# Five planner entries in an attention and two-layer feed-forward kernel: s rows ahead, v fetches later, small steps not held, sum fetches counted longer, A groups normalised ahead

## The chip, the cores and the metric

The kernel runs on one core of a Trainium2 chip. The metric is the device time of one execution in microseconds (us). Three runs of the kernel before gave 1052.65, 1056.55 and 1058.98 us; their median is 1056.55 us.

## The reference

Attention over 4 batches, 8 heads, 576 positions of 64 elements, with a causal mask and a bias from a running sum of `s`; its output, 2304 tokens by 512, goes through two gated feed-forward layers (512 to 1536 to 512), the first behind an RMS normalisation.

```python
cum  = np.cumsum(np.maximum(s, 0.0), axis=-1)
bias = -(cum[:, :, :, None] - cum[:, :, None, :])
scores = np.where(causal, -1e9, scale * q @ k.T + np.minimum(bias, 0.0))
attn = softmax(scores)                      # sum + 1e-9 in the denominator
x = (attn @ v), heads side by side          # 2304 x 512
xn = x / sqrt(mean(x * x) + 1e-6) * rms_g
h  = silu(xn @ w_gate) * (xn @ w_val);      x1 = h @ w_out
h2 = silu(x1 @ w2_gate) * (x1 @ w2_val);    out = h2 @ w2_out
```

## The kernel before, in words

**One planner writes every queue.** The kernel does not issue its instructions as it goes through its loops. Each `op(engine, ns, fn, r, w, pri, ...)` only records one instruction (or a few) with a planned duration, the buffers it reads and writes, and a priority. At the end `Plan.run` goes through a planned time: each time an engine is free, it takes the ready operation with the lowest `pri` number, and the order that comes out is the order of that engine's queue on the chip. On the chip each engine works through its queue strictly in that order and waits on semaphores, however the real times differ from the planned ones. So an entry that changes in one place can move other instructions of the same engine. The engines are TensorE (PE), VectorE (DVE), ScalarE (ACT), GpSimd (POOL) and SyncE (SP, which issues nearly all DMAs). Four entries matter here:

- `pri`: the rank. Attention unit number u has about `pri` u; its loads have u - 1000, and weight fetches of row f have 8 + 1.5 f - 1000. Matmuls of the first feed-forward layer have 10000 and more, so that they fill PE where attention leaves it free.
- `later`: planned ns by which the operation is held after what it depends on, unless that is a DMA.
- `slow`: for a DMA, ns that are added to its planned landing.
- `port`: a DVE operation with it is not planned to run while POOL runs one, nor does POOL begin one while it runs.

**The early part.** The first 256 positions ("group A") of the eight heads of batch 0 and then of batch 1 are computed by sixteen small units (`EarlyUnit`, `attend_early`). Each unit fetches q and k (L879, 128 KB), from the fifth unit on also a row of the bias (L884, 1 KB, from `cumA`) and v (L891, 64 KB; the first four units' v come over ACT's queue). It has scores on PE (L899, with L905 for the first four), a minimum and its column on DVE (L690), an exponent on ACT (L701), transposes (L917), a copy (L922 or L923) and the product with v (L927), copied to `x` (L932 or L933). There are four places for q and k and four for v, so unit u's fetches wait for unit u - 4. Weight fetches of the first layer (`raw`, L434, 512 KB each, two for each of the twelve rows of weights) share SP's queue; ACT, DVE and POOL turn what they bring into two halves H and L (L438, L440, L445 or L446, L449).

**Normalising a group.** When the eight heads of a group are in `x`, `normalise` squares them and sums the squares (L958, L965 in the early part; L958 to L991 later, where the squares are split and `split` is true), then comes a chain of small DVE operations on columns of 128 x 2 to 128 x 24 (helper `step`, L998; operations L1020 to L1054, of which the 18 from L1023 on form one chain: 6, then three rounds of 3, then 3), then transposes (L1058), a broadcast by matmul (L1066), the product (L1070) and the split into H and L (L1073, L1075). These are what the gate and value matmuls of the first layer (L1086) read, 24 for each row of weights and group.

**Later.** Batches 0 and 1 follow with their other positions ("group B"), batches 2 and 3 with both groups (`attend`, `units` numbered on). At their end `normalise` is called for each group with the rank of the last unit, less 1.0 for group A, less 2 inside. The second matmul of each layer is done by a scheme of seven products on sums of blocks. The sums of the first layer's rows are made by `sums_of_rows`: for each of six steps and two pairs of batches four fetches of h_d (L1365), four subtractions on DVE (L1370) and four stores (L1373).

Of the kernel before, what the change touches and what calls it, by code (L numbers as in the profile page):

```python
# [40 lines left out]
PE, DVE, ACT, POOL, SP, NONE = "PE", "DVE", "ACT", "POOL", "SP", "NONE"  # L41
# [38 lines left out]
class Plan:  # L80
# [20 lines left out]
    def op(self, eng, ns, fn, r=(), w=(), pri=0.0, later=0, port=False, slow=0.0):  # L101

        n = len(self.ops)
        done = 0
        if eng == SP:  # L110
            took = ns / self.RATE
            ns = max(450.0, took)
            done = 2300.0 + took - ns + slow
        deps, shared = set(), []
        for accesses, writes in ((r, False), (w, True)):
            for a in accesses:
                buf, part = a if isinstance(a, tuple) else (a, None)
                key = buf if isinstance(buf, str) else buf.key
                live = self.live.setdefault(key, [])
                keep = []  # L120
                for part2, m, wrote in live:
                    meets = part is None or part2 is None or part == part2
                    if meets and (writes or wrote) and m != n:
                        deps.add(m)
                    if not (writes and meets and (part is None or part == part2)):
                        keep.append((part2, m, wrote))
                keep.append((part, n, writes))
                self.live[key] = keep
                if not isinstance(buf, str) and buf.share is not None and buf not in shared:
                    shared.append(buf)  # L130
                    buf.uses += 1
        engs = eng if isinstance(eng, list) else [(eng, ns)]
        self.ops.append((engs, fn, deps, pri, done, shared, later, port))
        return n
# [160 lines left out]
TINY = 70  # L295
# [5 lines left out]
def tile_kernel(  # L301
# [16 lines left out]
    op = plan.op  # L318
# [83 lines left out]
    P_CONV, P_MOE, P_ATT = -1.0e3, 1.0e4, 0.0  # L402
# [72 lines left out]
    cumA = buf("at", "pTB1", [P, 2 * P], F32, "cumA")  # L475
# [372 lines left out]
    class EarlyUnit(Unit):  # L848
# [28 lines left out]
        def load(self, pri):  # L877
            ql, i = self.ql
            op(SP, 8 * D * 256, lambda en: en.dma_start(  # L879
                out=ql()[0:D, :, 288 * i:288 * i + 256], in_=qk[self.b, self.h, 0:D, :, 0:256]),  # L880
               w=self.parts[:2], pri=pri)
            n = self.b * NH + self.h
            if not self.first:
                op(SP, 1024, lambda en: en.dma_start(  # L884
                    out=ql()[D:D + 1, 1, 288 * i:288 * i + 256], in_=cumA()[n:n + 1]),
                   r=[cumA, self.rows], w=self.parts[2:], pri=pri, later=1000)
            if self.first:
                op(ACT, 450, lambda en: en.dma_start(
                    out=self.v(), in_=vp[self.b, self.h, :, 0:2]), w=[self.vl], pri=pri - 1e6)
            else:  # L890
                op(SP, 512 * P, lambda en: en.dma_start(  # L891
                    out=self.v(), in_=vp[self.b, self.h, :, 0:2]), w=[self.vl], pri=pri)

        def scores(self, pri):
            for t in self.tiles:
# [44 lines left out]
    def normalise(i, g, tot, pri, split=True):  # L940
# [3 lines left out]
        x = xbuf[i]  # L944
# [11 lines left out]
        for k in range(KD):  # L956
# [3 lines left out]
               r=[(x, (k, 0)), (x, (k, 64))], w=[q], pri=pri)  # L960

            if not split:
                def sums(en, q=q, k=k):
# [9 lines left out]
                    out=qh()[:, :n], in0=q()[:, :n], scalar1=1.0, scalar2=1.0, op0=ALU.mult,  # L973
                    op1=ALU.mult)}, r=[q], w=[qh], pri=pri)
            op([(DVE, c_tt(n)), (POOL, c_ptt(n))], 0, lambda en, q=q, qh=qh: en.tensor_tensor(
                out=sqL()[:, :n], in0=q()[:, :n], in1=f32(qh()[:, :n]),
                op=ALU.subtract), r=[q, qh], w=[sqL], pri=pri, port=True)
# [6 lines left out]
        if split:  # L984
# [3 lines left out]
               r=[ps], w=[sq[0]], pri=pri)  # L988
            ps2 = mo_bank()
            for c in range(nt):  # L990
                op(PE, C_TR, lambda en, c=c: en.transpose(  # L991
                    ps2()[:, c * P:c * P + P], sq[0]()[:, at[c]:at[c] + P], ident()),
                   r=[sq[0], ident], w=[ps2], pri=pri)
# [3 lines left out]

        def step(fn, r=(), w=None):  # L998
            w = [col] if w is None else w
            op(DVE, TINY, fn, r=[*w, *r], w=w, pri=pri, port=True)  # L1000

        def m():
            return col()[:, 0, :nt]
# [30 lines left out]
        for _ in range(3):  # L1034
# [6 lines left out]
            out=over(), in0=over(),  # L1041
# [118 lines left out]
    def attend(b, gs, xs):  # L1160

        tots = [totals[2 + b] if b < 2 else totals[2 * (b % 2) + x] for x in xs]
        for pair in range(NH // 2):
            heads, last = [], []
            for z in range(2):
                h = 2 * pair + z
                hd = Head(b, h, S, 0 if "A" in gs else 256)
                heads.append(hd)
                for g, x, tot in zip(gs, xs, tots):
                    units.append(hd)  # L1170
                    pri = P_ATT + len(units) - 1
                    if g == gs[0]:
                        hd.load(pri - 1000)
                        hd.prep_qk(pri - 0.5)
                        hd.prep_v(pri - 0.4)
                    u = Unit(hd, g, x, tot)
                    if g == "A":
                        u.scores(pri)
                        u.values(pri + 0.4)
                        continue  # L1180
                    last.append(u)
                    if z:
                        both = PairTile(heads, tot3[b % 2])
                        both.load(pri - 1000)
                        both.scores(pri - 0.1)
                    u.scores(pri)
            both.turn(pri + 0.1)
            last[0].values(pri + 0.2)
            both.second(pri + 0.3)
            last[1].values(pri + 0.4)  # L1190
        both.sums(tots[-1], P_ATT + len(units))
        for g, x, tot in zip(gs, xs, tots):
            normalise(x, g, tot, P_ATT + len(units) - (1.0 if g == "A" else 0.0))

    attend_early(0, 0, totals[0])
    attend_early(1, 1, totals[1])
# [157 lines left out]
    def h_rows(gi, f):  # L1354
        return [(f"h_d{gi}", (f, lo)) for lo in sorted(h_parts[gi])]
# [3 lines left out]
    def sums_of_rows(p, k, pri, after=()):  # L1359

        n = 512
        b11, b12, b21, b22 = t_bufs
        for t, gi, f in ((b11, 2 * p, k), (b12, 2 * p + 1, k), (b22, 2 * p + 1, k + K6),
                         (b21, 2 * p, k + K6)):
            op(SP, 4 * P * n, lambda en, t=t, gi=gi, f=f: en.dma_start(out=t(), in_=h_d[gi][f]),  # L1365
               r=[*h_rows(gi, f), *after], w=[t], pri=pri, later=2000)
        for i, (out, a, b) in enumerate(((b11, b12, b11), (b12, b22, b12), (b22, b22, b11),
                                         (b21, b21, b22))):
            op(DVE, c_tt(n) + 60, lambda en, out=out, a=a, b=b:
               en.tensor_tensor(out=out(), in0=a(), in1=b(), op=ALU.subtract), r=[a, b], w=[out],  # L1370
               pri=pri, port=True)
            name = ("T1", "T3", "T2", "T4")[i]
            op(SP, 4 * P * n, lambda en, out=out, name=name: en.dma_start(  # L1373
                out=t_d[p, name][k], in_=out()), r=[out], w=[(f"t{p}{name}", k)], pri=pri)
# [527 lines left out]
```

## Time and profile before

| what | value |
|---|---|
| median of three runs | 1056.55 us |
| profiled execution, its own time | 1057.39 us |
| its span | 1055.6 us |
| mean granted TensorE clock | 0.997 |
| PE / DVE / ACT / POOL busy | 99% / 73% / 61% / 26% of the span |
| DMA moved | 211.17 MB, 200 GB/s on average |

The span runs from the first instruction to the last. Busy is the time in which an engine has an instruction at work; a matmul's end is modelled. The granted clock is the share of TensorE's full clock (2.4 GHz); 0.50 is 1.2 GHz. A letter q after an engine (SPq) is its issuing part. "L899" is a line of the kernel.

### The profile page before, as it was taken

To read this page: it belongs to the slowest core of one execution; us is meant where nothing else is said; L and a number is where in the kernel's file an instruction comes from. 1 tells how busy PE (TensorE), PEld (TensorE's weight loads), DVE (VectorE), ACT (ScalarE), POOL (GpSimd) and SP (SyncE) were. 2 spreads that over 40 slices of the span, in tenths; PEclk is the share of its full clock that TensorE was granted. 3 is DMA by queue.
4 is the path that set the end of the run, shared out by engine and by line. 5 is a ranking of instruction groups with operands and counts; after the bars stand their busy time and mean duration, and the time that the engine had idled before them with its cause. 6 is when DMAs were issued, how large, how long until landed. Compare 5 with 4: busy or idle time off the path is not lost.

```text
span 1055.6 us, 19496 instructions
## 1 busy us (share of the span) xinstructions
PE 1040.2 (99%) x6322; PEld 937.2 (89%) x6322; DVE 771.7 (73%) x1880; ACT 641.5 (61%) x1373; POOL 273.5 (26%) x370
## 2 busy tenths in 40 slices
PE   8899999999999999999999999999999999999998
PEld 6599999999999999999988889888888888888888
DVE  7699788777777776757779887665667766976462
ACT  6689778867664775333466865555556444665652
POOL 4368556544343542000000000212122221300000
PEclk9899999999999999999999999999999999999999
DMA  7797555534546732666697662666667667888673
GB/s 204 229 282 221 144 150 148 164 117 128 158 142 204 246 106 85 188 208 206 206 299 244 197 222 84 222 210 220 228 202 256 219 232 263 292 259 261 207 244 105
DMA packets 127959, 211.17 MB, mean 200 GB/s; under 512 B 16176, under 2 KB 55600, under 8 KB 127856
## 3 DMA queue, kind: packets, MB, share of 16 engines
q1 hardware_dynamic: 126656, 209.32, 62.8%
q8 instruction: 50, 0.82, 0.3%
q10 hardware_dynamic: 1200, 0.60, 0.2%
q14 instruction: 53, 0.43, 0.1%
HBM read 145.29 MB, written 64.56 MB: 199 GB/s over the span
## 4 chain that ended last, share of the span: by engine, by line
PE 79%; DMA 7%; DVE 6%; ACT 3%; issue 3%; POOL 1%; SPq 1%; ACTq 0%; POOLq 0%; DVEq 0%
PE mo L1086 21%; PE mo L1455 8%; PE mo L1626 8%; PE sps L1626 6%; PE tp L1455 6%; PE sps L1455 5%; PE tp L745 4%; PE tp L733 3%; PE sps L664 2%; PE mo L1702 2%; DMA raw<-in_w_gv 2%; PE sps L1086 2%; PE tp L1086 2%; PE mo L1510 2%; DMA lq<-cumA 1%
## 5 line engine op out<-in xcount | busy, mean ns | idle before, releaser
L1086 PE MATMUL mo<-xL,H 128*128 128x256 f32 (+1 forms) x672 | 201.8, 300 | 0.1
L1086 PE MATMUL mo<-xH,H 128*128 128x256 f32 (+1 forms) x672 | 200.7, 300 | 0.3
L1086 PE MATMUL mo<-xH,L 128*128 128x256 f32 (+1 forms) x672 | 200.2, 298 | 0.0
L1351 DVE TENSOR_TENSOR hL<-hh,hH 128x512 fp32r<-128x512 f32 (+1 forms) x192 | 125.2, 662 | 67.1 <-ACT hH L1348 66.4
L1348 ACT ACTIVATE hH<-hh 128x512 fp32r<-128x512 f32 (+1 forms) x192 | 115.2, 603 | 91.6 <-DVE hL L1351 21.3
L1086 PEld LDWEIGHTS mo<-xL,H 128*128 128x128 f32 x672 | 127.0, 189 | 1.0 <-POOL xL L1075 0.5
L1086 PEld LDWEIGHTS mo<-xH,H 128*128 128x128 f32 x672 | 126.7, 189 | 1.1 <-ACT xH L1073 0.6
L1086 PEld LDWEIGHTS mo<-xH,L 128*128 128x128 f32 x672 | 126.9, 189 | 0.2
L701 ACT ACTIVATE sc<-sc,col 128x128 f32<-128x128 f32 (+3 forms) x128 | 73.2, 572 | 48.4 <-DVE col L690 46.1
L1455 PE MATMUL mo<-hH,wo 128*128 128x512 f32 x312 | 97.8, 389 | 0.0
L1455 PEld LDWEIGHTS mo<-hH,wo 128*128 128x128 f32 x312 | 58.6, 188 | 12.2
L1455 PE MATMUL mo<-hL,wo 128*128 128x512 f32 x156 | 61.1, 391 | 0.2 <-DVE hL L1351 0.2
L1455 PE MATMUL tp<-hH,wo 128*128 128x512 f32 x192 | 60.4, 389 | 0.0
L1093 ACT ACTIVATE t<-mo 128x256 f32<-128x256 f32 (+1 forms) x84 | 33.9, 403 | 43.4 <-PE mo L1086 43.3
L1632 ACT ACTIVATE u<-sps 128x512 f32<-128x512 f32 x48 | 28.5, 593 | 50.6 <-PE sps L1626 48.8
L745 PE MATMUL tp<-pTB,vst 128*128 128x320 f32 (+2 forms) x320 | 52.2, 294 | 1.6 <-ACT pTB L736 1.0
L1455 PE MATMUL sps<-hH,wo 128*128 128x512 f32 x168 | 52.9, 389 | 0.0
L1095 DVE SCALAR_TENSOR_TENSOR t<-t,mo 128x256 f32<-128x256 f32 (+1 forms) x84 | 37.8, 450 | 19.4 <-ACT t L1093 19.1
L738 DVE TENSOR_TENSOR pTB<-tp,pTB 128x512 fp32r<-128x512 f32 x64 | 44.0, 687 | 8.3 <-ACT pTB L736 7.2
L745 PEld LDWEIGHTS tp<-pTB,vst 128*128 128x128 f32 x320 | 46.5, 189 | 3.6 <-ACT pTB L736 1.7
L1589 POOL TENSOR_TENSOR tmp<-x,x 128x512 f32<-128x512 f32 x2 | 2.9, 1454 | 178.5 <-DVE x L1471 178.5
L733 PE MATMUL tp<-ident,sc 128*128 128x128 f32 x304 | 46.9, 274 | 0.6 <-DVE x L754 0.4
(289 smaller groups left out, 2925.9 us busy)
## 6 DMA issues: line engine op xcount, KB each, us to landing
raw<-in_w_gv SPq DMA_DIRECT2D x44, 511.8 KB, 5.4
tb<-h_d SPq DMA_DIRECT2D x48, 256.0 KB, 3.9
t<-tb SPq DMA_DIRECT2D x48, 256.0 KB, 2.4
hh<-t SPq DMA_DIRECT2D x48, 256.0 KB, 3.1
lq<-in_qk SPq DMA_DIRECT2D x32, 288.0 KB, 3.6
cb<-cum_d SPq DMA_DIRECT2D x32, 288.0 KB, 3.9
hh<-h_d SPq DMA_DIRECT2D x36, 256.0 KB, 3.6
h_d<-hh SPq DMA_DIRECT2D x54, 128.0 KB, 2.3
```

The lines of the kernel that those rows point to most:

```text
L701: op(ACT, c_act(o + m, 2) + 35, lambda en: en.activation(sc()[:m, :o + m], sc()[:m, :o + m], ACTF.Exp, scale=-1.0, bias=col()[:m, 0, t:t + 1],
L733: op(PE, C_TR, lambda en, pt=pt, a=a, kb=kb, t=t: en.transpose(pt()[:, a * P:a * P + P], self.sc[t]()[:, kb * P:kb * P + P], ident()), r=[ ...
L738: op(DVE, c_tt(n), lambda en, pt=pt, c=c: en.tensor_tensor(out=place(L, c), in0=source(pt, c), in1=f32(place(H, c)), op=ALU.subtract), r=[ ...
L745: op(PE, c_mm(n), lambda en, w=w, z=z, kb=kb, d0=d0, n=n, o=o: en.matmul(po()[:, o:o + n], vst[j]()[:, kb, :], pT[g][z]()[:, d0:d0 + n], s ...
L1086: op(PE, c_mm(n), lambda en, a=a, x=x, c=c, k=k, i=i: en.matmul(ps()[:, :n], a()[:, c], x()[:, k, :n], start=(k == 0 and i == 0), stop=(k ...
L1093: op(ACT, c_act(n), lambda en: en.activation(t()[:, :n], gp()[:, :n], ACTF.Tanh, scale=0.5), r=[gp], w=[t], pri=pri)
L1095: op(DVE, c_tt(n), lambda en: en.scalar_tensor_tensor(out=t()[:, :n], in0=t()[:, :n], scalar=1.0, in1=gp()[:, :n], op0=ALU.add, op1=ALU.mu ...
L1348: op(ACT, c_act(n) + 35, lambda en: en.activation(H(), src(), ACTF.Copy), r=[src, *after], w=[H], pri=pri)
L1351: lambda en: en.tensor_tensor(out=L(), in0=src(), in1=f32(H()), op=ALU.subtract),
L1455: op(PE, c_mm(n), lambda en, m=m, w=w, xx=xx, kk=kk, i=i: en.matmul(ps[m]()[:, :n], w(), xx(), start=first and kk == 0 and i == 0, stop=kk ...
L1626: op(PE, c_mm(n), lambda en, w=w, xx=xx, cut=cut, kk=kk, i=i: en.matmul(ps()[:, :n], W[w]()[:, cut], xx(), start=first and kk == 0 and i == 0,
L1632: op(ACT, c_act(n), lambda en: en.activation(dst(), ps()[:, :n], ACTF.Copy), r=[ps], w=[dst], pri=-1.0e4)
```

## The change

Five entries of the planner's records change; no instruction does.

```diff
--- before.py
+++ after.py
@@ EarlyUnit.load
                 op(SP, 1024, lambda en: en.dma_start(
                     out=ql()[D:D + 1, 1, 288 * i:288 * i + 256], in_=cumA()[n:n + 1]),
-                   r=[cumA, self.rows], w=self.parts[2:], pri=pri, later=1000)
+                   r=[cumA, self.rows], w=self.parts[2:], pri=pri - 3, later=1000)
...
                 op(SP, 512 * P, lambda en: en.dma_start(
-                    out=self.v(), in_=vp[self.b, self.h, :, 0:2]), w=[self.vl], pri=pri)
+                    out=self.v(), in_=vp[self.b, self.h, :, 0:2]), w=[self.vl], pri=pri + 2.2, later=800)
@@ normalise, step
-            op(DVE, TINY, fn, r=[*w, *r], w=w, pri=pri, port=True)
+            op(DVE, TINY, fn, r=[*w, *r], w=w, pri=pri, port=split)
@@ attend
-            normalise(x, g, tot, P_ATT + len(units) - (1.0 if g == "A" else 0.0))
+            normalise(x, g, tot, P_ATT + len(units) - (4.0 if g == "A" and len(gs) > 1 else 0.0))
@@ sums_of_rows
             op(SP, 4 * P * n, lambda en, t=t, gi=gi, f=f: en.dma_start(out=t(), in_=h_d[gi][f]),
-               r=[*h_rows(gi, f), *after], w=[t], pri=pri, later=2000)
+               r=[*h_rows(gi, f), *after], w=[t], pri=pri, later=2000,
+               slow=2500)
```

The row of the bias of early unit u now ranks with the q and k of unit u - 3, and its v with those of unit u + 2.2, held for 800 ns after the place is free. The two early groups are normalised with `split` false, so their small steps lose `port`; the later groups keep it. Group A of batches 2 and 3 is normalised with a rank three units lower. Each fetch of `sums_of_rows` has a planned landing 2.5 us later.

## Rows read from the trace of the kernel before

**Rows 1.** The page, busy us, share of the span and instructions of TensorE.
```profile
PE 1040.2 (99%) x6322; PEld 937.2 (89%) x6322; DVE 771.7 (73%) x1880; ACT 641.5 (61%) x1373; POOL 273.5 (26%) x370
```

**Rows 2.** Windows: stretch, length, busy us (instructions) by engine, clock, DMA share, GB/s.
```profile
26.00:53.00 27.00, 23.07 (x118) 15.96 (x119) 19.08 (x73) 17.79 (x53) 8.22 (x9) 0.87 0.74 230
...
38.30:45.10 6.80, 6.79 (x21) 4.49 (x22) 2.67 (x12) 2.08 (x8) 1.94 (x2) 0.50 0.53 154
45.10:51.20 6.10, 5.45 (x36) 3.97 (x34) 5.39 (x17) 4.96 (x14) 1.59 (x2) 1.00 0.99 344
...
53.00:73.00 20.00, 19.72 (x154) 18.76 (x152) 18.66 (x57) 18.37 (x42) 12.18 (x14) 1.00 0.89 275
73.00:93.00 20.00, 19.63 (x154) 19.08 (x155) 19.19 (x61) 17.86 (x42) 16.53 (x22) 1.00 0.74 242
...
280.00:300.00 20.00, 18.77 (x134) 17.97 (x133) 16.01 (x63) 13.48 (x35) 8.56 (x15) 1.00 0.60 173
```

**Rows 3.** Chain of waits: start us, us, what the chain goes through.
```profile
31.70 6.48 DMA lq<-cumA
...
63.61 8.25 DMA raw<-in_w_gv
...
286.08 5.96 DMA tb<-h_d
```

**Rows 4.** Timeline of PE, 33 to 52 us: start, us, instruction, idle before.
```profile
38.31 0.77 PE L899 MATMUL sps<-lq 128*128 128x128 f32 x2 [2.48 <-DMA lq<-cumA]
...
44.30 1.25 PE L927 MATMUL tp<-pTA,vl 128*64 128x256 f32 x4
...
51.24 0.57 PE L1086 MATMUL mo<-xH,H 128*128 128x256 f32 x2
```

**Rows 5.** Timeline of SP, 28 to 44 us: DMAs in order of issue.
```profile
29.91 0.43 SPq L434 DMA_DIRECT2D raw<-in_w_gv  x1
30.38 0.55 SPq L879 DMA_DIRECT2D lq<-in_qk  x1
31.33 0.33 SPq L891 DMA_DIRECT2D vl<-in_vp  x1
```

**Rows 6.** DMA issues at 30.40 and at 31.35 us: KB, us to landing.
```profile
lq<-in_qk SPq DMA_DIRECT2D x1, 128.0 KB, 7.3
...
vl<-in_vp SPq DMA_DIRECT2D x1, 64.0 KB, 6.6
```

**Rows 7.** Timeline of DVE: small steps of normalise, first, second and a later group.
```profile
30.22 0.17 DVE L1023 TENSOR_TENSOR fac<-mo,fac 128x16 f32<-128x16 f32 x1
...
35.10 0.16 DVE L1038 SCALAR_TENSOR_TENSOR rc<-rc 128x2 f32<-128x2 f32 x1
...
48.07 0.18 DVE L1054 TENSOR_TENSOR sq<-fac,sq 128x16 f32<-128x16 f32 x1
...
66.75 1.25 DVE L1028 TENSOR_SCALAR rc<-rc 128x2 f32<-128x2 f32 x1
...
91.06 0.27 DVE L1054 TENSOR_TENSOR sq<-fac,sq 128x16 f32<-128x16 f32 x1
...
321.49 0.18 DVE L1023 TENSOR_TENSOR fac<-mo,fac 128x24 f32<-128x24 f32 x1
...
325.55 0.18 DVE L1054 TENSOR_TENSOR sq<-fac,sq 128x24 f32<-128x24 f32 x1
```

**Rows 8.** Timeline of POOL, 61 to 92 us.
```profile
66.54 1.43 POOL L619 TENSOR_TENSOR kLL<-lq,kHH 128x576 fp32r<-128x576 f32 x1
```

**Rows 9.** Timeline of PE, 305 to 331 us: transposed factors, then broadcast.
```profile
306.53 0.38 PE L1058 MATMUL mo<-ident,sq 128*128 128x128 f32 x2
...
326.33 0.96 PE L1066 MATMUL mo<-xL,sel 128*128 128x256 f32 x4
```

**Rows 10.** Waits of SP, 26 to 60 us, and DVE: us, times, longest.
```profile
SPq L891 <- PE tp L927: 2.5, 1, 2.5
...
DVE tb L1370 <- DMA tb<-h_d: 5.5, 5, 2.3
```

## The prediction

> **What bounds the kernel now.** I read the page's busy times first, then the windows by stage, then the chain of waits, then the timelines of single engines where the chain leaves TensorE. TensorE (PE) is busy 1040.2 of the 1055.6 us of the span [rows 1], so an edit can only gain where PE is idle, where its matmuls are few, or where its clock is low. The windows say where that is: from 53 to 73 us PE has 19.72 busy us in 20 with 154 matmuls, but from 26 to 53 us only 23.07 in 27 with 118, and the granted clock there is 0.87 [rows 2]. The first 53 us are the early part: sixteen short units of attention (eight heads of batch 0, eight of batch 1), a latency chain with nothing to fill PE beside it, since the first gate/value matmul (L1086) comes only at 51.24 us [rows 4]. From there PE is full, and whatever moves PE work ahead of 51 us shortens the whole run by the same amount as long as PE stays full behind it.
>
> Three things hold that part up. The chain of waits shows a row of s that is issued at 31.70 us and takes 6.48 us to land [rows 3]; PE stands still for 2.48 us until it is there and starts again at 38.31 us [rows 4]. From 38.30 to 45.10 us the granted clock is then 0.50 [rows 2], that is 1.2 GHz instead of 2.4, after the stall and a stretch of few matmuls. And the group of eight heads that is complete at 30 us is normalised only at 48 us: its 18 small VectorE (DVE) steps begin at 30.22 us, the twelfth of them runs at 35.10, the last at 48.07 [rows 7]. Later PE is idle in one more place that the diff touches: 1.23 us between 280 and 300 us [rows 2], where the chain has a fetch of h_d that takes 5.96 us [rows 3].
>
> **The change part by part.** No instruction is added or removed; five entries of the planner change, so what changes is the order of each engine's queue. I work against the profiled execution, 1057.39 us (span 1055.6 and 1.8 around it), which is 0.84 above the median of the runs, 1056.55.
>
> *Small early steps not held back (port=split).* So far the planner let no such step begin while it had GpSimd (POOL) at work, nor the other way round. The same chain of steps with POOL idle shows what it takes unheld: from 321.49 to 325.55 us, 4.1 us from first to last [rows 7]. In the early part other DVE work lies between, and the first twelve took 4.9 us; at that pace all 18 take some 7.3 us and end near 37.5 us instead of 48.2. Behind the last step the matmuls began 3.2 us later (48.07 to 51.24), so the first would come near 41 us, ten earlier. What that is worth: between 38.30 and 51.20 us PE did 21 + 36 = 57 matmuls [rows 2]; at the rate of the next stage (154 in 20 us, 0.13 us each) it would be 99. 42 matmuls are 5.5 us; from 41 us on, 10.2 of the 12.9 us, it is 4.3. I take **-4.0**, bounds 0 (the steps stay behind the units' own DVE work) and -5.5. The second group's chain, which ends only at 91.06 us [rows 7], shortens as well, but PE is full there (idle 0.28 of 20 us from 53, 0.37 from 73) [rows 2]: **-0.5**, bounds 0 and -0.65.
>
> What it costs: a step may now meet a POOL operation. One did already: at 66.75 us a step of L1028, a tiny operation like those of 0.16 us, took 1.25 us, and ended with the POOL subtraction of L619 that ran from 66.54 for 1.43 us [rows 7, 8]. DVE works in order, so the next scores of the units stand behind such a step. At worst all 18 meet one so: 18 x 1.1 = 20 us of DVE time a group; at best the order before already paid as much, and nothing is lost. I take 0, since the other steps in these rows took 0.16 to 0.27 us, and the planner's times, by which the hold works, drift from the chip's anyway; this stays a rival below. The Trainium skill (SBUF — State Buffer, "Who interferes with whom") states this as a lock: a DVE instruction with two SBUF inputs, or in a two-port mode, and a POOL instruction that reads SBUF exclude each other, the later one waiting for the whole of the earlier. The row of L1028 agrees with it. By that rule, with POOL busy 8.22 of 27 us before 53 us and 16.53 of 20 us from 73 [rows 2], a third to five sixths of the steps are held up, by half a POOL operation (0.7 us), an estimate of 4 to 11 us of DVE a group; if a quarter of that reached PE, the sum below would be -5 to -3 instead of -6.
>
> *Rows of s ahead (pri - 3), v later (+2.2 and 800 ns).* Twelve rows of 1 KB and twelve fetches of v of 64 KB on SP's queue change places among themselves and with the weight fetches (raw, 512 KB). The queue's order shows in [rows 5]: a weight fetch at 29.91, the q/k of the unit that stalls at 30.38, a v at 31.33, then the row at 31.70. A row ahead of that v would still stand behind the weight fetch, and so does q/k, which lands 7.3 us after its issue [rows 6], at 37.7 us: only 0.5 us before the row (38.18). The fetch of weights ranks ahead of this q/k before and after the change. So the stall of 2.48 us shrinks by 0.5, not by all: **-0.5**, bounds 0 and -2.5 (the weight fetch itself slips behind).
> A v whose slot is not yet free blocks SP, and the weight fetches behind it: 2.5 us in one case between 26 and 60 us [rows 10]. A later v lets those fetches pass. The price is a v that lands late. The v of 31.33 us lands 6.6 us later [rows 6], at 37.9, and its unit's value matmuls begin at 44.30 [rows 4]: 6.4 us of cover, 3 us less if the units run ahead by that much. One weight fetch put ahead costs what the spacing of landings shows, at most the 6.5 us of a whole landing. I take 0, bounds 0 and +3.
>
> *Longer fetches counted for first sums (slow=2500).* The 24 + 24 fetches of h_d get a planned landing 2.5 us later, so their subtractions (L1370) are placed later in DVE's queue. DVE waited for them 5.5 us in all, 2.3 at the longest [rows 10], and that once is behind the fetch of 5.96 us, where PE ran dry: all idle time of that window is 1.23 us [rows 2]. I take **-1.0**; bounds -1.23 and +0.8 (buffers are held longer, and another fetch is late instead). The sums are needed from 521 us, so their delay is covered.
>
> *Late first groups normalised ahead (-4 for -1).* Two groups have it, batches 2 and 3. The first shows why it is worth nothing: its factors are transposed at 306.53 us, yet its broadcast (L1066) starts at 326.33 [rows 9], because the matmuls of the earlier batch still read the tiles it writes. Ranked three units higher it waits longer at the same place. **0**, bounds -0.8 and +0.8 (it holds one of four PSUM banks earlier).
>
> Sum: -4.0 - 0.5 - 0.5 - 1.0 = -6.0, so 1057.4 - 6.0 = **1051.4 us**. If PE were short of work behind 51 us the early gain would be given back; 53 to 93 us says it is not.
>
> **The rivals.**
> *Given back.* Matmuls that start ten us earlier need weights, and the chain has a wait for a weight fetch at 63.61 us, 8.25 us long [rows 3]. For it: one megabyte is wanted for each pair of matmul rows, and the DMA share is 0.89 from 53 to 73 us [rows 2]. Against it: PE was idle only 0.28 us there, and the second group, normalised sooner, lets each weight serve twice. Then only the sums and the 0.5 us of the row are left, less some reordering: 1054.5 to 1058, say 1056.
> *The edit doesn't reach the chip.* The stall at 38 us comes from transfers that the planner takes to be quicker than they are, and steps planned behind the stalled unit's scores stand still with it. Then the last six steps end where they did, about 47 us, and the gain is 1 to 2 us: 1055.5.
> *Slower: v behind weight fetches.* In its place in SP's queue a v finds one or two weight fetches ahead; its unit's value matmuls stand at PE's head, and all behind them waits. It decides when a v lands later than its transposes are done, so when the cover of 6.4 us is used up: 3 us by faster units, the rest by a fetch (4 to 6.5 us). One such stall would be like the one seen: 2.5 us, and the clock falls again, 6.8 us at half for up to 3.4 us. If the old stall also stays, 1057.4 + 5.9 - 1.0 = 1062. Against it: one v in twelve has to be hit so, and with moving matmuls as fill the clock need not fall.
> *Slower, by DVE.* Each blocked small step (1.1 us) delays the units' scores; between 53 and 93 us DVE is busy 18.66 and 19.19 of 20 us [rows 2], so ten such blocks are 10 us of that stage's DVE. PE has fill meanwhile, and so only a part counts: 1058 to 1062.
>
> **How the numbers follow.** Forecast, 1048 to 1054.5: 0.52. Given back or not reached, 1054.5 to 1059: 0.27. The two slower rivals, 1059 to 1064: 0.14. More than forecast (also the 2.48 us stall gone and the clock not fallen), below 1048: 0.07. The range 1046 to 1060 leaves out the upper half of the slow cases and the best of the good ones. A measurement of this kernel tells about 0.5% from no change: faster ends at 1051.3 us, slower begins at 1061.8. The forecast lies on the first bound; of its case somewhat over two thirds lie under it, since the bounds of the largest term reach further down: faster 0.44, same 0.45, slower 0.11.
>
> **What would show it.** Right: the last small step of the first group before 40 us and the first L1086 matmul near 41; no 0.50 clock after 42 us; more than 57 matmuls between 38.3 and 51.2; the wait for the row gone or near 2 us; no long wait of DVE for tb (L1370). Wrong: L1086 still starts near 50 us; PE waits for vl (L927) anywhere before 60 us; small steps of more than 1 us in numbers; PE idle over 0.6 us in 20 between 53 and 93 us; gaps behind 300 us that were not there.

## The result, and the profile after

The changed kernel takes 1067.56 us (median of six runs, 1063.62 to 1068.64), the kernel before 1054.17 beside it: ratio 1.0113, 95% interval 1.0087 to 1.0139. The forecast of 1051.4 had the wrong sign, and the time lies outside its range. The profiled execution took 1068.64 us, 11.25 more than that of before. From the page, TensorE's busy time:

```profile
PE 1045.5 (98%) x6322; PEld 941.4 (88%) x6322; DVE 788.3 (74%) x1887; ACT 643.0 (60%) x1376; POOL 263.1 (25%) x360
```

The same 6322 matmuls; the busy time grew by 5.3 us [rows 1], some 3 us of it because more of them ran at half clock (the mean granted clock was 0.994 instead of 0.997; an estimate), and the rest of the 11.25 us is idle time. The windows say where (columns as in [rows 2]; the stretches of that group first, then three longer ones):

```profile
26.00:53.00 27.00, 25.08 (x138) 18.65 (x137) 20.15 (x79) 19.96 (x63) 8.94 (x11) 0.87 0.74 212
38.30:45.10 6.80, 6.50 (x25) 4.95 (x26) 2.48 (x12) 2.93 (x9) 2.75 (x3) 0.61 0.91 286
45.10:51.20 6.10, 6.10 (x38) 4.97 (x37) 5.02 (x15) 5.34 (x17) 3.16 (x5) 0.88 0.50 147
53.00:73.00 20.00, 19.32 (x145) 17.75 (x143) 18.46 (x43) 14.36 (x33) 11.16 (x13) 1.00 0.87 277
73.00:93.00 20.00, 15.72 (x109) 15.00 (x108) 19.65 (x59) 15.78 (x37) 12.40 (x17) 0.91 0.79 237
...
53.00:106.00 53.00, 46.90 (x344) 44.14 (x343) 50.60 (x129) 40.35 (x93) 33.80 (x40) 0.97 0.76 233
106.00:350.00 244.00, 241.51 (x1795) 236.43 (x1794) 195.65 (x670) 173.31 (x437) 113.96 (x184) 1.00 0.52 149
540.00:600.00 60.00, 57.71 (x251) 46.32 (x250) 48.64 (x78) 38.99 (x70) 1.30 (x1) 1.00 0.79 258
```

The same three long stretches of the kernel before, and one that is used below:

```profile
53.00:106.00 53.00, 52.35 (x409) 50.57 (x408) 50.30 (x158) 47.67 (x112) 40.76 (x50) 1.00 0.81 252
106.00:350.00 244.00, 241.52 (x1802) 236.76 (x1801) 188.35 (x656) 170.78 (x433) 116.88 (x188) 1.00 0.51 151
540.00:600.00 60.00, 59.98 (x263) 49.00 (x263) 51.17 (x82) 40.16 (x71) 1.30 (x1) 1.00 0.78 248
...
350.00:1050.00 700.00, 699.07 (x3865) 615.72 (x3864) 493.96 (x921) 386.55 (x722) 94.92 (x97) 1.00 0.66 213
```

Ahead of 53 us the change did a little of what the forecast says: 25 + 38 = 63 matmuls between 38.3 and 51.2 us instead of 57. Behind it, from 53 to 106 us, PE does 65 fewer; at 0.13 us each that is 8.5 us. It is idle 6.1 us there (53 - 46.90) instead of 0.65, while DVE is as busy as before. Between 540 and 600 us another 2.3 us are lost.

TensorE's timeline of the changed kernel: the stalled unit, the first transposed factors, the first gate/value matmul, and the longest stall behind it (in brackets the idle time before and what ended it):

```profile
38.60 0.46 PE L899 MATMUL sps<-lq 128*128 128x128 f32 x2 [1.92 <-DMA lq<-in_qk]
...
44.92 0.64 PE L1058 MATMUL mo<-ident,sq 128*128 128x128 f32 x2
...
49.39 0.47 PE L1086 MATMUL mo<-xH,H 128*128 128x256 f32 x1
...
76.31 0.41 PE L664 MATMUL sps<-kHH,qst 128*128 128x384 f32 x1 [3.04 <-DVE col L690]
```

The stall at 38 us is 1.92 instead of 2.48 us [rows 4] and now waits for q and k, as the forecast said. L1086 starts 1.9 us earlier, not ten. The stall at 76 us is new. DVE's and POOL's timelines show what stood before it: DVE's last small step of the first group, then three of the second, and POOL beside these:

```profile
40.93 0.17 DVE L1054 TENSOR_TENSOR sq<-fac,sq 128x16 f32<-128x16 f32 x1
...
71.62 1.27 DVE L1032 TENSOR_SCALAR rc<-rc 128x2 int32<-128x2 int32 x1
...
73.62 0.82 DVE L1037 TENSOR_TENSOR rc<-rc 128x2 f32<-128x2 f32 x1
...
74.71 1.08 DVE L1038 SCALAR_TENSOR_TENSOR rc<-rc 128x2 f32<-128x2 f32 x1
```

```profile
71.43 1.43 POOL L619 TENSOR_TENSOR kLL<-lq,kHH 128x576 fp32r<-128x576 f32 x1
73.40 1.03 POOL L628 TENSOR_TENSOR vst<-vl,vst 128x320 fp32r<-128x320 f32 x1 [0.53 <-DMA raw<-in_w_gv]
74.48 1.29 POOL L449 TENSOR_TENSOR L<-raw,H 128x512 fp32r<-128x512 f32 x1
```

Each of the three steps began while a POOL operation ran and ended within 0.03 us of it (72.89 and 72.86, 74.44 and 74.43, 75.79 and 75.77). Unheld, such a step takes 0.17 us [rows 7]; the three lost 1.10 + 0.65 + 0.91 = 2.7 us, and the scores that PE waited for stood behind them in DVE's queue. That the later of the two waits for the whole of the other is what the Trainium skill says (SBUF — State Buffer, "Who interferes with whom"); the three pairs agree. It is the rival "Slower, by DVE". But the kernel before, whose steps are held in the plan, has four such steps in the same stage, that of 66.75 us [rows 7] and these three, each ended within 0.03 us of a POOL operation:

```profile
74.74 0.97 DVE L1037 TENSOR_TENSOR rc<-rc 128x2 f32<-128x2 f32 x1
...
80.56 0.83 DVE L1038 SCALAR_TENSOR_TENSOR rc<-rc 128x2 f32<-128x2 f32 x1
...
87.97 0.63 DVE L1053 CAST sq<-fac 128x16 fp32r<-128x16 f32 x1
```

They cost DVE 3.0 us, and PE was idle only 0.65 us there. So the plan's hold does not keep the steps apart from POOL on the chip, and a blocked step alone is not a stall of PE. The experiments ask what is.

### The profile page after: what moved, and what is told of

It is laid out like the page before. It is cut to its first block, busy times and chain, and to the rows that moved or that the text cites. A ratio compares the mean times of both kernels' runs of the same rounds, so it can differ in the third digit from the quotient of the medians.

```text
span 1066.8 us, 19453 instructions
## 1 busy us (share of the span) xinstructions
PE 1045.5 (98%) x6322; PEld 941.4 (88%) x6322; DVE 788.3 (74%) x1887; ACT 643.0 (60%) x1376; POOL 263.1 (25%) x360
## 4 chain that ended last, share of the span: by engine, by line
PE 75%; DVE 5%; DMA 4%; ACT 2%; issue 2%; POOL 0%; ACTq 0%; SPq 0%; DVEq 0%; POOLq 0%
PE mo L1086 19%; PE mo L1627 10%; PE sps L1627 8%; PE mo L1456 7%; PE sps L1456 4%; PE tp L1456 4%; PE tp L745 4%; PE mo L1703 3%; PE tp L733 2%; PE sps L664 2%; PE sps L1086 2%; PE tp L1086 2%; PE mo L1511 2%; PE tp L1627 1%; DMA hh<-t 1%
## 5 line engine op out<-in xcount | busy, mean ns | idle before, releaser
L1086 PE MATMUL mo<-xH,H 128*128 128x256 f32 (+1 forms) x672 | 201.5, 302 | 0.8 <-ACT xH L1073 0.5
L1086 PE MATMUL mo<-xL,H 128*128 128x256 f32 (+1 forms) x672 | 202.1, 301 | 0.2
L1086 PE MATMUL mo<-xH,L 128*128 128x256 f32 (+1 forms) x672 | 201.1, 299 | 0.0
L1086 PEld LDWEIGHTS mo<-xH,H 128*128 128x128 f32 x672 | 127.2, 190 | 2.1 <-ACT xH L1073 1.4
L1086 PEld LDWEIGHTS mo<-xL,H 128*128 128x128 f32 x672 | 127.7, 190 | 0.9 <-POOL xL L1075 0.6
L1086 PEld LDWEIGHTS mo<-xH,L 128*128 128x128 f32 x672 | 127.5, 190 | 0.3 <-issue 0.2
L619 POOL TENSOR_TENSOR kLL<-lq,kHH 128x576 fp32r<-128x576 f32 x28 | 41.0, 1465 | 28.1 <-ACT kHH L612 27.2
```

The lines of the kernel that those rows point to most:

```text
L619: op([(POOL, c_ptt(n)), (DVE, c_tt(n))], 0, lambda en: en.tensor_tensor(out=kl()[:, :n], in0=ql()[:, :n], in1=f32(kh()[:, :n]), op=ALU.sub ...
L1086: op(PE, c_mm(n), lambda en, a=a, x=x, c=c, k=k, i=i: en.matmul(ps()[:, :n], a()[:, c], x()[:, k, :n], start=(k == 0 and i == 0), stop=(k ...
```

## The experiments

Each ratio is against the kernel before, on the same chip; it is not the ratio of the two medians. The theories, in the order in which they came up:

- **A.** The second group's unheld steps collide with POOL, and PE runs dry.
- **B.** A transfer comes late: v behind weight fetches. **B2.** Or the rows, put ahead, hold up others.
- **C, C2.** The edits make the planner draw a new order for all engines (a redraw), and the new order fits the chip less well.
- **D.** Attention, paced by DVE, sets the end; work of the first layer brought ahead leaves PE dry later.
- **E, F.** A new order costs where DVE has no time to spare (53 to 106 us), or anywhere before 350 us.

| kernel | median us | ratio and interval | PE busy 53 to 106 us | PE places changed, of 321 |
|---|---|---|---|---|
| before | 1054.2 to 1055.3 | 1 | 52.35 | 0 |
| after | 1067.56 | 1.0113 [1.0087, 1.0139] | 46.90 | 211 |
| e1 small steps alone | 1060.15 | 1.0054 [1.0033, 1.0074] | 50.26 | 215 |
| e2 the same, first group only | 1062.81 | 1.0076 [1.0054, 1.0099] | 49.04 | 128 |
| e3 rows and v | 1068.28 | 1.0125 [1.0092, 1.0158] | 50.08 | 123 |
| e4 the two late edits | 1056.75 | 1.0019 [1.0000, 1.0037] | 51.93 | 0 |
| e5 rows | 1063.04 | 1.0064 [1.0042, 1.0087] | 51.34 | 97 |
| e6 v | 1068.04 | 1.0100 [1.0071, 1.0129] | 48.05 | 165 |
| e7 all but v | 1063.47 | 1.0069 [1.0042, 1.0096] | 49.46 | 225 |
| e8 control, order kept | 1054.85 | 0.9987 [0.9964, 1.0010] | 52.06 | 1 |
| e9 v late, other engines' order of before | 1058.10 | 1.0027 [1.0005, 1.0049] | 52.36 | 0 |
| e10 v early, order of e6 | 1063.82 | 1.0080 [1.0052, 1.0109] | 48.08 | 165 |
| e11 redraw, no edit | 1072.59 | 1.0160 [1.0130, 1.0191] | 46.82 | 146 |
| e12 redraw, no edit | 1066.27 | 1.0106 [1.0075, 1.0137] | 50.36 | 173 |
| e13 rows ahead, order of before | 1055.69 | 1.0015 [0.9996, 1.0034] | 52.55 | 0 |
| e14 redraw from 120 us | 1057.26 | 1.0034 [1.0018, 1.0050] | 52.24 | 0 |
| e15 redraw, mostly from 100 us | 1058.43 | 1.0041 [1.0022, 1.0059] | 52.00 | 22 |
| e16 after, short splits on DVE | 1063.12 | 1.0093 [1.0066, 1.0119] | 48.73 | 211 |
| e17 early work slid 5.3 us | 1073.00 | 1.0168 [1.0144, 1.0193] | 49.14 | 139 |
| e18 slid 2.5 us | 1068.25 | 1.0131 [1.0109, 1.0153] | 49.48 | 134 |

The last column counts the operations of PE that the plan of before has between 60 and 100 us and that a diff of its whole order of PE with the new one leaves out.

**e1 to e4: the parts by themselves.** The diffs are the lines of the change; e2 holds the second group's steps back again:

```diff
-            op(DVE, TINY, fn, r=[*w, *r], w=w, pri=pri, port=True)
+            op(DVE, TINY, fn, r=[*w, *r], w=w, pri=pri, port=split or i == 1)
```

> The kernel before with one entry changed: the small steps of the two early groups lose port. Theory A (the steps of the second group are planned beside POOL, meet it on the chip, are held up for whole POOL operations, and PE runs dry behind the stalled DVE): slower by 5 to 10 us, and between 65 and 85 us small steps of 0.6 to 1.3 us with a PE gap of 1 us or more behind them. Theory B (the fetches of rows and v did it): within 3 us of before. Theory C (the loss is spread over stages, as each entry draws a new order everywhere): slower by 0 to 5 us, with no single gap over 1 us after 55 us.

> Only the first early group's steps lose port; the second group's keep it. Theory A: the loss of the run before this one goes, within 3 us of the kernel before or faster; no small step over 0.6 us between 65 and 85 us more than before had. Theory B: within 3 us as well. Theory C: a value of its own, slower or faster by up to 5 us, unrelated to the second group's steps. By the prediction's sum: faster by about 4 us.

> Only the rows of s ahead and the early v later. Theory A: within 3 us of before. Theory B: slower by 6 to 10 us, with PE waits for lq or vl before 60 us. Theory C: slower by 0 to 5 us.

> Only the two late entries: group A normalised ahead, the fetches of h_d counted longer. Theory A: within 2 us of before (the early part is as before), the changed kernel's stall of some 2.3 us near 564 us may stand here too and then costs 2 to 3 us. Theory B: the same. Theory C: slower by 0 to 5 us.

Held again in the second group, the steps give nothing back, but e2 does not part them from POOL: seven of them take over 0.5 us between 53 and 106 us (four before, five in the changed kernel, two in e1). A falls as the cause of the loss since their number does not go with it: e12 below has four, like the kernel before, and loses 1.06%. The parts cost 0.54, 1.25 and 0.19%, together 1.98, more than the 1.13% of the whole, so they are not separate costs that add up. In e4 PE is fuller at the place of the slow fetches, as the forecast says, and idle later; its windows, against 18.77 [rows 2] and, in the kernel before, 40.00 busy us of 40 in the second:

```profile
280.00:300.00 20.00, 19.69 (x139) 18.74 (x138) 17.86 (x70) 15.11 (x42) 8.60 (x16) 1.00 0.59 180
...
520.00:560.00 40.00, 38.51 (x167) 30.71 (x166) 31.02 (x50) 24.31 (x42) 0.00 (x0) 1.00 0.86 279
```

Both differences shrink beside e8, e9 and e13, which have the order of before there: 19.20 to 19.22 busy us in the first window, 39.28 to 39.73 in the second.

**e5 to e8: rows, v, all but v, and a control** in which only a planned duration of DVE changes, by too little to reorder anything:

```diff
-TINY = 70
+TINY = 71
```

> Only the rows of s rank three units ahead (pri - 3); everything else as before. Theory B (the loss comes from v, which ranks 2.2 units later and so finds two to four weight fetches of 512 KB more ahead of it): 1052 to 1057, ratio 0.998 to 1.003, last v of the early units issued near 42 us and the last early value matmul (L927) begins near 55 us as before. Theory B2 (the rows put the q/k fetches behind them and slow the units): 1061 to 1066, ratio above 1.006. Theory C (any entry that redraws the planner's order costs some 5 us): 1057 to 1061 whatever the edit.

> Only v is changed (rank + 2.2, held 800 ns). Theory B: 1062 to 1069, ratio 1.008 to 1.014; the last two v land at 52 and 59 us where before they landed at 39.7 and 44.1, and the last L927 begins at 61 to 63 us instead of 55. Theory B2: 1052 to 1057. Theory C: 1057 to 1061.

> The whole change without its edit of v. Theory B: the loss of the v edit goes and the rest stays; alone, the small steps cost 0.5%, the two late edits 0.2%: 1055 to 1060, ratio 1.001 to 1.005, against 1.0113 of the whole change; last L927 at 55 to 57 us. Theory B2: still 1064 to 1069. Theory C: about 1060.

> A control: the planned duration of the smallest DVE operations is 71 ns instead of 70; no rank, hold or fetch is changed, but the planner's tie breaks and so parts of each queue's order are redrawn. Theories B and B2 (a named transfer is late): 1052 to 1057, ratio 0.998 to 1.003, with the last early v issued near 42 us. Theory C (every redrawn order costs): 1057 to 1061, ratio 1.003 to 1.007.

Read alone, e6 confirms B, e5 B2, and e8 seems to rule out C. But e8 is no control for C: its order is that of before. What e8 does show is that a kernel with the order of before takes as long as before.

e7 shows more: it has the front that the forecast wanted. The first group's last small step ends at 38.1 us, the first gate/value matmul begins at 42.92 us, and the clock is full up to 53 us. e4 has nearly as full a front for another reason: its plan is that of before up to 228 us, and its profiled execution ran without the stall at 38 us and the half clock behind it. Windows of the kernel before, of e7 and of e4:

```profile
0.00:53.00 53.00, 45.62 (x241) 32.70 (x242) 37.95 (x145) 35.51 (x106) 20.91 (x36) 0.94 0.75 217
53.00:350.00 297.00, 293.87 (x2209) 287.33 (x2208) 238.65 (x813) 218.46 (x544) 157.64 (x237) 1.00 0.56 169
...
0.00:53.00 53.00, 48.76 (x284) 36.95 (x285) 43.34 (x149) 40.58 (x118) 21.94 (x40) 1.00 0.79 233
53.00:350.00 297.00, 290.18 (x2157) 282.11 (x2156) 244.92 (x805) 216.67 (x536) 145.32 (x227) 1.00 0.54 162
...
0.00:53.00 53.00, 47.82 (x278) 35.62 (x279) 42.77 (x155) 40.02 (x117) 22.23 (x38) 1.00 0.80 234
53.00:350.00 297.00, 294.93 (x2225) 289.12 (x2224) 240.91 (x820) 219.09 (x547) 157.28 (x240) 1.00 0.55 167
```

At 53 us e7 is 43 matmuls ahead of the kernel before and e4 37. At 350 us e4 is 53 ahead, and e7 nine behind. So in these executions the lead is kept with the order of before and lost with the new one; D would lose e7's as well.

**e9 and e10: the transfer and the order, crossed.** In e9 PE, DVE, ACT and POOL have the order of before, and on SP the v stand about as late as in e6; in e10 the engines have the order of e6, and the v stand early. Both change the planner's finished order, by a list AT of places for the twelve early v:

```diff
         out.sort()
+        at = {n: t for t, _, n, _ in out}
+        for n, t in zip(self.moved, AT):
+            low = max(at[m] for m in ops[n][2]) + 0.5
+            high = min(at[u] for u in users[n]) - 0.5
+            at[n] = min(max(t, low), high)
+        out = sorted((at[n], k, n, e) for _, k, n, e in out)
```

> The order of before on PE, DVE, ACT and POOL, instruction for instruction; on SP alone the twelve early v are put where the v edit put them (the last two at places 53 and 61 of SP's order instead of 46 and 51, behind two to four more weight fetches). Theory B (the late v costs the time): 1061 to 1069, ratio 1.006 to 1.013, PE waits for vl (L927) near 50 and 56 us for several us. Theory C2 (the loss comes from the order that the planner redraws on the other engines between 60 and 350 us, which fits the chip less well): 1053 to 1059, ratio below 1.004.

> The converse: the order that the v edit gives on PE, DVE, ACT and POOL, but on SP the twelve v stand where they stood before. Theory B: the loss is gone, 1052 to 1058, ratio 0.998 to 1.003. Theory C2: it stays, 1062 to 1068, ratio 1.006 to 1.012.

The stall that the late v makes in e9:

```profile
47.02 1.09 PE L937 MATMUL tp<-pTA,vl 128*64 128x256 f32 x4 [1.92 <-DMA vl<-in_vp]
```

The window of e10, in which PE does 54 matmuls fewer than before:

```profile
53.00:106.00 53.00, 48.08 (x355) 44.54 (x354) 49.22 (x138) 39.40 (x91) 34.73 (x45) 1.00 0.75 227
```

The late v makes its stall, 1.92 us (L937 is L927 shifted by ten lines), and costs 0.27%; PE is as full behind it as before. The new order costs 0.80% with the v in time, and PE is as empty as in e6. So B holds for about a quarter of e6's loss, C2 for the rest.

**e11 and e12: redraws without any edit.**

```diff
-           (DVE, DVE): 127, (DVE, ACT): 125, (DVE, PE): 245, (DVE, POOL): 203,
+           (DVE, DVE): 127, (DVE, ACT): 125, (DVE, PE): 247, (DVE, POOL): 203,
...
-C_TR = 110
+C_TR = 112
```

> A control that does redraw: the planner takes 247 instead of 245 ns from DVE to PE; no rank, hold or fetch is changed, but 146 of 307 matmul entries of its plan between 60 and 100 us and 240 of 735 between 150 and 250 us change place, about as many as with each edit of the change. Its own total is 1030.9 us against 1030.5. Theory B (named transfers are late): no loss, 1052 to 1058, ratio 0.998 to 1.003. Theory C2 (any redrawn order costs): 1058 to 1065, ratio 1.003 to 1.010.

> A second one: a transpose is planned with 112 instead of 110 ns; 173 of 321 matmul entries of the plan between 60 and 100 us change place, 375 of 735 between 150 and 250 us; the planner's own total is 1032.0 us (+1.4). Theory B: 1053 to 1059. Theory C2: 1058 to 1066, ratio 1.003 to 1.010.

A planned latency that is 2 ns longer costs 1.6%, at least as much as the change. Waits of PE between 53 and 106 us, longest groups (us in all, times, longest), first before, then e11, where its window has 46.82 busy us:

```profile
PE tp L745 <- DVE pTB L819: 0.3, 1, 0.3
PE tp L745 <- DVE pTB L738: 0.2, 1, 0.2
PE tp L745 <- ACT pTB L736: 0.2, 1, 0.2
```

```profile
PE tp L745 <- DVE pTB L738: 4.0, 1, 4.0
PE sps L789 <- DVE col L690: 0.9, 1, 0.9
PE mo L1086 <- POOL xL L1075: 0.5, 1, 0.5
```

In the order of before, PE finds its attention matmuls ready; in e11's, as in the changed kernel at 76 us, it comes to one whose DVE operation isn't done. And e11 and e12 had no work ahead that could be missing later: 235 and 228 matmuls up to 53 us (before 241), the first gate/value matmul at 53.17 and 54.00 us. D may stand beside C2 in e7, but it does not explain these two.

**e13 to e16.** e13 is e9's edit for the rows (their places on SP alone). e14 has `LAT_DMA = 135` for 130, e15 `SLACK = 1510.0` for 1500. e16 has the whole change and its order, but the low halves of q and k that DVE computes are cut to 32 columns for heads 2 to 15 (the rest of them is left out):

```diff
...
+            op([(POOL, c_ptt(w)), (DVE, c_tt(w))], 0, {POOL: low(QW), DVE: low(c0 + 32 if self.light else QW)},
...
```

> The order of before on PE, DVE, ACT and POOL; on SP alone the twelve early rows of s stand where the edit of the rows puts them. The edit itself cost 0.64%. Theory C2 (the redrawn order of the other engines costs, not the transfers): the loss is gone; the stall of 2.5 us before 38 us shrinks by 0.5 to 1.5 us and perhaps the half clock behind it goes: 1050 to 1055, ratio 0.996 to 1.001. Theory B2 (rows ahead hold up the fetches behind them): 1058 to 1064, ratio above 1.003.

> A redraw that leaves the plan as it was until about 120 us (a transfer's release is planned with 135 instead of 130 ns; 0 of 321 matmul entries change place between 60 and 100 us, 39 of 403 to 150, 240 of 735 to 250 us, 232 of 738 to 350; planned total 1030.3 against 1030.5 us). Theory E (what a new order costs it costs where DVE has no time to spare, 53 to 106 us): 1053 to 1058, ratio 0.998 to 1.003. Theory F (it costs wherever the order is redrawn, before 350 us): 1059 to 1066, ratio 1.004 to 1.012.

> A small redraw (a matmul that waits for another engine is held 1510 instead of 1500 ns in the plan): 2 of 178 matmul entries change place between 30 and 60 us, 22 of 321 to 100, 125 of 403 to 150, 243 of 735 to 250 us; planned total 1030.5 us as before. Theory E: a small loss, 1053 to 1059, ratio 0.998 to 1.004. Theory F: 1059 to 1066.

> The whole change with its order on every engine, but where the planner gave the low halves of q and k (L616, L619) to DVE, heads 2 to 15 compute only 32 columns of them there (the rest of the low half is left out). In the changed kernel these two lines have 6.5 us of DVE between 53 and 106 us, against 2.1 in the kernel before, where POOL does them. Theory E (DVE's load in 53 to 106 us is what PE waits for): PE busy in 53 to 106 us rises from 46.9 to over 49.5 us, the wait of 3.0 us for col (L690) at 76 us goes, time 1057 to 1062. If DVE's load is not it: PE busy below 48 us and 1064 to 1068.

e13: the loss of the rows is the order's as well (0.64% with it, 0.15% without, an interval that holds no change). e14 and e15: orders that stay as they were up to 120 us, or nearly so up to 100 us, lose 0.34 and 0.41%, a fifth to two fifths of the full redraws. Windows of e14, its first gate/value matmul and its longest waits of PE behind 350 us:

```profile
26.00:53.00 27.00, 25.61 (x165) 19.26 (x163) 24.62 (x87) 23.34 (x66) 10.09 (x11) 1.00 0.87 266
350.00:1050.00 700.00, 695.81 (x3836) 612.07 (x3835) 493.49 (x909) 384.57 (x716) 84.35 (x86) 1.00 0.64 210
...
45.66 0.58 PE L1086 MATMUL mo<-xH,H 128*128 128x256 f32 x2
...
PE mo L1626 <- ACT u L1632: 1.9, 3, 1.5
PE sps L1626 <- ACT u L1632: 0.9, 2, 0.7
```

This execution did not have the stall before 38 us nor the half clock: 165 matmuls from 26 to 53 us instead of 118 [rows 2], and L1086 5.6 us earlier, with the order of before. All engines came ahead together, PE stayed as full behind (table), and at 298 us the pair tile's scores (L789) were still 4.2 us ahead (293.77 against 297.96). So the redraw between 120 and 300 us cost little here. From 350 us on, where PE idles 0.93 us in the kernel before, it idles 4.2, and 2.8 of that are waits in the second layer (L1626): the planner redrew 48 of 984 operations between 700 and 900 us as well. That is nearer to E, but e14 does not test it cleanly.

That a lead is kept where the order stays shows in the times too. Of the 95 executions of the kernel before beside e1 to e18, the 25 with a mean granted clock of 0.999 or 1 took 1052.6 us on average, the 26 with 0.996 or less 1057.7. In the profiled one the clock was below full in the first 53 us alone.

e16 is inconclusive: of the 6.5 us that these two lines (L616, L619) have on DVE from 53 to 106 us in the changed kernel, 5.6 are left, and the interval overlaps that of the whole change. PE's stall there is shorter, 2.1 instead of 3.0 us.

**e17 and e18: the forecast's main term alone, in intent.** The plan of before, in which only the first group's normalisation and the first layer's work (matmuls and what follows them) are put earlier, by up to 5.3 or 2.5 us, tapering to nothing at 330 us, where their inputs allow it:

```diff
+            far = max(0.0, 1.0 - max(0.0, t - self.FROM) / (self.TO - self.FROM))
+            if n in self.moved and far > 0.0:
...
+                at[n] = min(t, max([t - self.SLIDE * far, *low]))
```

> The forecast's main term by itself, with no rank, hold or duration changed: the plan of before, in which the first group's normalisation and the matmuls of the first layer with what follows them are put up to 5.3 us earlier (as much as the small-steps edit moved them), tapering to nothing at 330 us; attention keeps its own order. The forecast's step (whatever moves PE work ahead of 51 us shortens the run): first L1086 near 46, PE does over 60 matmuls in 38.3 to 51.2 us, time 1049 to 1053, ratio 0.995 to 0.999. Theory D (attention, paced by DVE, sets the end, and work brought ahead leaves PE dry later): first L1086 as early, PE busy in 53 to 106 us under 51.5 us, time 1054 to 1060, ratio 1.000 to 1.006.

> The same with 2.5 instead of 5.3 us. The forecast's step: 1051.5 to 1054. Theory D: 1053.5 to 1058, between the kernel before and the longer slide.

Windows of e17, and its first gate/value matmul (L1121 there):

```profile
38.30:51.20 12.90, 11.04 (x65) 7.51 (x64) 11.68 (x37) 9.38 (x28) 4.75 (x5) 1.00 0.80 244
53.00:106.00 53.00, 49.14 (x371) 45.99 (x371) 44.94 (x143) 45.77 (x105) 38.05 (x46) 1.00 0.79 245
106.00:350.00 244.00, 237.12 (x1730) 228.75 (x1730) 183.82 (x635) 165.90 (x421) 115.11 (x186) 1.00 0.50 144
...
47.45 0.61 PE L1121 MATMUL mo<-xH,H 128*128 128x256 f32 x2
```

The first matmul is 3.8 us earlier, and 65 matmuls stand between 38.3 and 51.2 us where 56 stood (57 as the sum of two windows). Then PE is emptier everywhere: 38 matmuls fewer from 53 to 106 us, 72 fewer from there to 350. The time is 1.7% longer, far outside what either theory gave. D has the direction, but e17 and e18 do not show it: up to 53 us e17 did 237 matmuls in all, no more than the 241 of before, and half the slide lost nearly as much as the whole. Their orders differ from that of before in 139 and 134 places, about as many as e11's, and they lose about as much, so they are not told apart from redraws without purpose. No kernel tried is faster than the one before.

## Why the prediction was wrong, point by point

- **The step that failed:** "whatever moves PE work ahead of 51 us shortens the whole run by the same amount as long as PE stays full behind it", with the last sentence on the sum, that 53 to 93 us says PE does. e7 has the forecast's front: 43 matmuls more than before up to 53 us (the forecast counted 99 - 57 = 42), the first L1086 at 42.92 us. From 53 to 350 us PE was then idle 6.8 instead of 3.1 us, the lead was gone, and the run took 0.69% longer. The full PE of [rows 2] belongs to one order of the queues. The edit changes that order, and in every order redrawn before 60 us that was timed PE is emptier behind 53 us. The sentence holds for a stall that goes while the order stays (e4, and the executions of the kernel before). The rival "Given back" had the place (behind 53 us), but named weights as its means and stopped at no gain.
- **No cost was put on the reordering.** The forecast speaks of places on one queue. The five entries moved 211 of the 321 PE operations planned from 60 to 100 us; redraws that move 146 and 173 without any purpose cost 1.6 and 1.1%. This is the larger share of what rows and v cost as well: 0.64% against 0.15% for the rows (e5, e13), 1.00% against 0.27% for v (e6, e9). For the small steps, the largest term, it is argued and not shown: no run moves them alone in the order of before.
- **Small steps, -4.0 and -0.5:** the last step began at 40.93 us, not near 37.5: the chain began 3.2 us later than before (33.45 against 30.22), and its third round stood behind a unit's copy that waited for the stalled PE. Then 8.5 us passed to L1086 instead of 3.2; PE had the units in front, with a granted clock of 0.61 up to 45.1 us. In e7, without the stall, the chain ended as the forecast says. The second group's last step began at 79.43 instead of 91.06 us, and PE was emptier there. The edit alone cost 0.54%, some 5.7 us (e1).
- **Rows ahead, -0.5:** the stall shrank by 0.56 us, as worked out, and in e13 to 1.7 us with L1086 no earlier (51.23 us); but this stall varies by more between executions (e14). **v later, 0 to +3:** a stall of 1.92 us in e9, 2.8 us in all: inside the bounds, and the rival's mechanism, at a quarter of the change's cost.
- **Slow fetches, -1.0:** PE's busy time from 280 to 300 us rose by 0.92 us (e4), as forecast, but e8, e9 and e13 have nearly half of that with the order of before. "The sums are needed from 521 us, so their delay is covered" is in doubt: 1.49 us of idle time between 520 and 560 in e4, up to 0.72 in those three.
- **Late A groups, 0:** not told apart from the slow fetches; the two cost 0.19% together, with an interval that begins at no change.
- **By DVE:** three blocked steps stand before a stall of 3 us. But the forecast took their cost as 0 from one case, where the kernel before has four, and the loss does not go with their number (e1: two, e12: four).

Two things stay open: which property of the order of before keeps PE full, and whether it is a rare good draw or work put ahead is missed later in any order (D). The splits' choice of engine, collisions of DVE and POOL, and the spacing of the first layer's matmuls all differ with each order, and e16 was too weak a dose.

## What to carry to other kernels

Where a planner writes in-order queues, an edit of one entry can be an edit of all of them: count first how many places change, and time a redraw without purpose before crediting or blaming a part. To test a part, move it in the finished order and keep the rest; a control has to change the order as much as the edit does. A full engine shows that this order feeds it, not that it would stay full with its work elsewhere.

## What was not expected of the hardware

The start differs from one execution to the next with the same order on every engine. The stall at the fifth unit and the clock behind it, in the kernel before and then in e8:

```profile
14.07 0.46 PE L899 MATMUL sps<-lq 128*128 128x128 f32 x2 [1.05 <-DMA lq<-cumA]
...
15.90:19.20 3.30, 3.09 (x18) 1.84 (x16) 2.80 (x9) 3.30 (x12) 1.30 (x1) 1.00 0.27 65
```

```profile
15.18 0.46 PE L899 MATMUL sps<-lq 128*128 128x128 f32 x2 [2.16 <-DMA lq<-cumA]
...
15.90:19.20 3.30, 3.30 (x12) 2.37 (x11) 0.75 (x5) 1.73 (x6) 1.29 (x1) 0.50 0.25 71
```

A stall 1.1 us longer, and 12 matmuls at half clock instead of 18 at full. Yet the two kernels have about the same median (1055.3 and 1054.85). So single executions of this program, which range from 1049.7 to 1061.4 us for the kernel before, can't be compared by their first 50 us alone. The stall at 38 us and the stretch of few matmuls behind it, from which the forecast took its largest term, are one draw too: e14, with the same order there, ran without them.
